# Six conversion steps per pair of heads: three and three between the halves, instead of two and four

## The chip, the cores and the metric

One core of one Trainium2 chip. The metric is the device time of one execution in microseconds (us); the kernel before takes 887.9 us. All runs of this study, of all kernels, agree with others of the same kernel to 0.3%, and none was in a slow state, so every comparison is between fast runs. Effects here are 0.1 to 0.7% of the time. I therefore read them twice: from timed runs, with an interval, and from intervals within the traces, which repeat far better (interval B, below, to about 0.04 us between kernels that should not differ in it).

## The reference

Attention whose mask comes from a hash, then a feed-forward layer:

```python
# q, k, v: (4, 8, 768, 64); proj: (64, 6)
q_bucket = number made of the 6 signs of q @ proj;  k_bucket likewise
scores = 0.125 * q @ k.T, masked (-1e9) where q_bucket != k_bucket
attn = softmax(scores);  x = (attn @ v) as (3072, 512)
# w_in: (512, 2048), w_out: (2048, 512), both float64
h = x @ w_in;  g = h / (1 + exp(-1.702 * h));  out = (g @ w_out).astype(float32)
```

`w_in` and `w_out` arrive as 64-bit numbers. The kernel computes in float32, so it turns each into a float32 number from its two 32-bit halves with a few operations: the "conversion" of this study. The reference computes in double precision there.

## The kernel before

The attention stage goes over 16 pairs of heads. Each pair is two groups, half c=0 and half c=1 of the queries. Of 16 chunks of `w_in` (128 x 512 numbers each), 14 are converted beside the attention, one in each of pairs 1 to 14, because VectorE has some time there; the last two are left to the feed-forward stage. In the traces VectorE and ScalarE take their operations in the order in which the program issues them: in the pair shown in the prediction, ScalarE begins the square L190 at 109.70, right behind L468, the operation before it in the program, though all that the square needs had been ready since 100.10. The parts that matter, cut:

```python
def convert(cv, dst, src, queue=None, psum=None):
    raw = cv.tile([P, CW, 2], U32, tag="raw", name="raw")
    (queue or loader[0]).dma_start(out=raw, in_=src)
    lo, hi = raw[:, :, 0], raw[:, :, 1]
    # ... here part is dst (SBUF) and size is hi, in place
    yield
    nc.vector.scalar_tensor_tensor(part, hi, 3, masks[0x3FFFFFFF], ...)          # L178
    yield
    nc.vector.scalar_tensor_tensor(bits, hi, 0xC0000000, part, ...)              # L182
    yield
    nc.vector.tensor_tensor(part, bits, masks[0xFF800000], op=Alu.bitwise_and)   # L186
    nc.scalar.activation(size, hi.bitcast(F32), Act.Square)                      # L190, ScalarE
    part = part.bitcast(F32)
    yield
    nc.vector.scalar_tensor_tensor(part, lo, 2.0**-52, part, ...)                # L193
    yield
    nc.vector.tensor_tensor(dst, of(bits.bitcast(F32)), of(part), op=Alu.add)    # L195
    yield
    nc.vector.scalar_tensor_tensor(dst, of(size), ..., dst, ...)                 # L198, needs the square
```

```python
def add_low(n, c):                       # GpSimd: the sum of exponentials 0 to 2
    nc.gpsimd.tensor_tensor(acc, es[c][:, 0, ...], es[c][:, 1, ...], op=Alu.add)  # L440
    nc.gpsimd.tensor_tensor(acc, acc, es[c][:, 2, ...], op=Alu.add)               # L441
def add_high(n, c):                      # VectorE: 3 to 5, and the other sum
    nc.vector.scalar_tensor_tensor(acc, e[0], T * TINY, e[1], ...)                # L446
    for x in (e[2], accs.pop((n, c, 0))):
        nc.vector.tensor_tensor(acc, acc, x, op=Alu.add)                          # L448
def unload(n, c):                        # ScalarE: av out of PSUM
    nc.scalar.copy(vs, av[:, HS : HS + 1])                                        # L467
    nc.scalar.activation(x_of(n)..., av..., Act.Identity, bias=vs[:, 0:1])        # L468
def total(n):                            # TensorE: denominators of both halves
    for c in range(2):
        acc = accs.pop((n, c))
        for j in range(2):
            nc.tensor.matmul(dn[r0 : r0 + 32, :], ones[:, 0:32], acc[:, j, :], ...)  # L477
# ... the loop over groups g = (n, c):
    scores(n, c, kts)                    # TensorE L432, exponentials on ScalarE L433
    if kts[0] == 0: add_low(n, c)
    if hashes: featured(hashes.pop())    # VectorE L413, then eight small transfers
    if ended: add_high(*prev[:2])
    for x in turned: turn(n + 1, x); measure(n + 1, x)   # in c=0
    while norms: norm(norms.pop(0))      # VectorE L497, in c=1
    ... total(), invert()                # in c=0: dn, then L484 to L492
    values(*prev)                        # TensorE L456, av
    if ended: unload(*prev[:2])
    if "q" in turned: hashed(n + 1)      # TensorE L408
    if kts and kts[-1] == T - 1:
        step(n, 2 + 2 * c)               # L576: the next steps of this pair's conversion
        if c == 0 and n > last - len(x_sums):
            x_sums[n - last - 1]()       # one 128 x 1024 operation in pairs 12 to 15
        if c == 1: begin(n + 1)          # load of the next chunk
```

## Time and profile before

| | before |
|---|---|
| median of the first 3 runs | 887.87 us |
| span in the profile | 885.6 us |
| TensorE / VectorE / ScalarE / GpSimd busy | 98% / 82% / 35% / 36% |
| attention stage (ends with the last `av`) | up to 330.6 us |

In the profile a line "L190" is a line of the kernel; PE is TensorE, DVE VectorE, ACT ScalarE, POOL GpSimd. A bracket at the end of a timeline line is the idle time of the engine before it, with what ended it. The lines on the steady state are in the prediction below. One stretch that it only mentions is shown here: the idle times of TensorE in pair 1, where the pipeline is still filling. Timeline of the kernel before, TensorE, columns start, duration, engine, line, operation, tiles, form:

```profile
52.53 0.84 PE L477 MATMUL dn<-acc,ones 128*32 128x384 f32 x4
54.91 0.84 PE L477 MATMUL dn<-acc,ones 128*32 128x384 f32 x4 [1.54 <-DVE acc L448]
```

Half of pair 1's denominators run at 52.53. The other half waits until VectorE ends its sum at 54.86, and so TensorE is idle for 1.54 us after the first half has ended.

### The profile page before, as it was taken

What the parts mean: (1) busy time and instruction counts of PE and PEld (TensorE: products, weight loads), DVE (VectorE), ACT (ScalarE), POOL (GpSimd) and SP (SyncE); (2) the same over time, 40 slices, a digit from 0 to 9 for tenths busy, and PEclk for the clock granted to TensorE, in tenths of its full rate; (3) what the DMA queues carried; (4) which work ended last, traced back from release to release, by engine and by line L of the source; (5) the groups of instructions that cost most, each with busy time, mean ns of one, the idle gap of its engine ahead of it and who ended that gap; (6) DMA issues with size and microseconds to landing.
All of it is one profiled execution on the core that took longest, in us unless ns stands there. A gap on an engine that the chain in (4) does not pass through costs nothing.

```text
span 885.6 us, 11940 instructions
## 1 busy us (share of the span) xinstructions
PE 869.4 (98%) x4077; PEld 501.0 (57%) x4077; DVE 723.3 (82%) x1020; ACT 309.2 (35%) x519; POOL 320.7 (36%) x275
## 2 busy tenths in 40 slices
PE   9999999999999999999999999999999999999995
PEld 5444444444444444444444444444888888888884
DVE  4599899999999965777778877888898977897785
ACT  5755666666656642223222223322000000000000
POOL 4244333433433363766434444559932000000000
PEclk9999999999999999999999999999999999999998
DMA  4754555566544103555455545575835665467524
GB/s 103 115 90 82 82 92 95 91 100 98 92 83 83 46 1 120 201 192 192 162 202 207 197 167 189 192 252 180 307 139 191 205 215 205 164 209 238 190 95 98
DMA packets 169477, 132.01 MB, mean 149 GB/s; under 512 B 123936, under 2 KB 138432, under 8 KB 164032
## 3 DMA queue, kind: packets, MB, share of 16 engines
q1 hardware_dynamic: 167712, 129.69, 51.5%
q10 hardware_dynamic: 1696, 1.48, 0.6%
q8 instruction: 34, 0.56, 0.3%
q14 instruction: 35, 0.29, 0.1%
HBM read 79.69 MB, written 50.33 MB: 147 GB/s over the span
## 4 chain that ended last, share of the span: by engine, by line
PE 96%; DVE 2%; ACTq 0%; ACT 0%; issue 0%; DVEq 0%
PE product L699 33%; PE product L812 28%; PE ps L432 17%; PE av L456 14%; PE dn L477 2%; PE hash L408 1%; PE tp L366 1%; DVE acc L448 0%; ACTq L420 0%; DVE xT L816 0%; PE warm L359 0%; PE hash L373 0%; DVE y L791 0%; DVE w_in_sb L193 0%; DVE w_in_sb L186 0%
## 5 line engine op out<-in xcount | busy, mean ns | idle before, releaser
L433 ACT ACTIVATE e<-ps 128x768 f32<-128x768 f32 x192 | 148.4, 811 | 23.5 <-PE ps L432 18.3
L432 PE MATMUL ps<-qT,kT 64*128 64x384 f32 x768 | 155.1, 482 | 0.0
L699 PE MATMUL product<-xT,w_in_sb 128*128 128x512 f32 x288 | 135.4, 592 | 0.0
L456 PE MATMUL av<-e,v 128*64 128x385 f32 x768 | 131.8, 490 | 0.9 <-ACT xT L468 0.9
L440 POOL TENSOR_TENSOR acc<-e 128x768 f32<-128x768 f32 x32 | 58.7, 1833 | 195.4 <-DVE acc L448 185.9
L707 ACT ACTIVATE c<-c 128x512 f32<-128x512 f32 x72 | 45.3, 630 | 186.4 <-issue 73.2
L456 PEld LDWEIGHTS av<-e,v 128*64 128x64 f32 x768 | 52.1, 136 | 77.6 <-issue 75.5
L699 PEld LDWEIGHTS product<-xT,w_in_sb 128*128 128x128 f32 x288 | 54.6, 190 | 68.5 <-issue 63.5
L699 PE MATMUL product<-t_x,s_in 128*128 128x512 f32 x192 | 90.2, 592 | 0.0
L432 PEld LDWEIGHTS ps<-qT,kT 64*128 64x128 f32 x768 | 68.2, 188 | 34.1 <-issue 32.9
L219 POOL TENSOR_TENSOR v<-c,u 128x512 f32<-128x512 f32 x24 | 34.2, 1423 | 127.5 <-ACT c L707 127.5
L818 ACT COPY u<-product 128x256 f32<-128x256 f32 x21 | 7.8, 372 | 168.0 <-PE product L812 125.8
L432 PE MATMUL ps<-qf,kf 64*128 64x384 bf16 x384 | 63.0, 324 | 1.3 <-ACT e L433 1.2
L699 PEld LDWEIGHTS product<-t_x,s_in 128*128 128x128 f32 x192 | 36.5, 190 | 45.9 <-issue 43.8
L441 POOL TENSOR_TENSOR acc<-acc,e 128x768 f32<-128x768 f32 x32 | 59.1, 1847 | 2.5
L699 PE MATMUL product<-t_x,w_in_sb 128*128 128x512 f32 x96 | 45.1, 592 | 0.0
L699 PE MATMUL product<-xT,s_in 128*128 128x512 f32 x96 | 45.1, 592 | 0.0
L432 PEld LDWEIGHTS <-kf 64*128 64x128 bf16 x384 | 20.1, 94 | 42.9 <-issue 21.4
L467 ACT COPY vs<-av 128x1 f32<-128x1 f32 x32 | 5.1, 159 | 91.1 <-PE av L456 91.1
L446 DVE SCALAR_TENSOR_TENSOR acc<-e 128x768 f32<-128x768 f32 x32 | 30.5, 953 | 7.7 <-ACT e L433 7.7
L812 PE MATMUL product<-raw_g,xT 128*128 128x256 f32 x152 | 35.1, 379 | 0.0
L448 DVE TENSOR_TENSOR acc<-acc,e 128x768 f32<-128x768 f32 x32 | 32.0, 999 | 2.4
(207 smaller groups left out, 1547.4 us busy)
## 6 DMA issues: line engine op xcount, KB each, us to landing
raw_g<-g_dram SPq DMA_DIRECT2D x22, 1024.0 KB
s_in<-g_dram SPq DMA_DIRECT2D x20, 1024.0 KB
g_dram<-c SPq DMA_DIRECT2D x72, 256.0 KB
g_dram<-t SPq DMA_DIRECT2D x48, 256.0 KB
raw<-in_moe_w_out_dram SPq DMA_DIRECT2D x16, 512.0 KB
raw<-in_moe_w_in_dram SPq DMA_DIRECT2D x15, 512.0 KB
v<-in_v_dram SPq DMA_DIRECT2D x32, 192.0 KB
g_dram<-u SPq DMA_DIRECT2D x24, 256.0 KB
```

What stands on the lines that cost most here:

```text
L219: return [lambda: eng.tensor_tensor(t1, b12, b11, op=Alu.subtract), lambda: eng.tensor_tensor(b12, b22, b12, op=Alu.subtract), lambda: eng ...
L432: nc.tensor.matmul(ps[:, j, 0:HS], a[hs, keys], m[hs, cols], start=not last, stop=last)
L433: nc.scalar.activation(es[c][:, kt, :, 0:HS], ps[:, :, 0:HS], Act.Exp, scale=1.0 / D**0.5)
L440: nc.gpsimd.tensor_tensor(acc, es[c][:, 0, :, 0:HS], es[c][:, 1, :, 0:HS], op=Alu.add)
L441: nc.gpsimd.tensor_tensor(acc, acc, es[c][:, 2, :, 0:HS], op=Alu.add)
L446: nc.vector.scalar_tensor_tensor(acc, e[0], T * TINY, e[1], op0=Alu.add, op1=Alu.add)
L448: nc.vector.tensor_tensor(acc, acc, x, op=Alu.add)
L456: nc.tensor.matmul(av[D * j : D * (j + 1), :], vt[:, t, j, :], es[c][:, t, j, :], start=(t == 0), stop=(t == T - 1))
L477: nc.tensor.matmul(dn[r0 : r0 + 32, :], ones[:, 0:32], acc[:, j, :], start=True, stop=True)
L699: nc.tensor.matmul(ps, wq[LEFT[i]][:, kc, :], xq[RIGHT[i]][:, kc, :], start=(kc == 0), stop=(kc == K2 - 1))
L707: nc.scalar.activation(c, c, Act.Gelu_apprx_sigmoid)
L812: nc.tensor.matmul(ps, wq[LEFT[i]][:, c, :], gq[RIGHT[i]][:, c, :], start=(c == 0), stop=(c == F4 - 1))
```

## The change

The half c=0 now takes three of the six remaining steps, and c=1 the other three. The intent is to share VectorE's work more evenly between the halves.

```diff
                 if kts and kts[-1] == T - 1:
-                    step(n, 2 + 2 * c)
+                    step(n, 3)
```

No work is added or removed. The third step holds L186 (VectorE) and L190 (ScalarE); these two move from c=1 to c=0, 14 times.

## The prediction

> **What bounds the kernel now.** I read the page first, for the engine that is never idle, then the chain of work that ended last, for the places where that engine is nevertheless late, then the waits, and last the timeline of one pair of heads (two groups: half c=1 of one pair, half c=0 of the next).
>
> ```profile
> PE   9999999999999999999999999999999999999995
> DVE  4599899999999965777778877888898977897785
> ```
>
> These are rows of the page, one digit per fortieth of the 885.6 us span. TensorE is full nearly everywhere. VectorE is almost full too, but only in slices 2 to 14, which is the attention stage (about 20 to 330 us) that the change touches. From 55 to 311 us the table by stages gives TensorE busy for all of every stretch, so no plain wait is left to take away there. What can be lost is hidden inside matmuls, so I compared equal groups along the chain:
>
> ```profile
> 34.99 0.78 PE dn L477 x8
> ...
> 54.91 0.84 PE dn L477 x4
> ...
> 113.94 0.97 PE dn L477 x8
> ...
> 311.45 1.13 PE dn L477 x8
> ...
> 342.79 0.78 PE dn L477 x8
> ```
>
> Columns: start, length on the chain in us, engine, tile, line, number. The same eight denominator matmuls (`dn`, once per pair) cost 0.78 us where nothing holds them and 0.96 to 1.14 us in pairs 2 to 14. The first four use the sum `acc` of half c=0, long ready; the other four use that of half c=1 and run beside them in other columns of the array, so a late second `acc` lengthens the group instead of showing as a gap. Why it is late, from the waits and the timeline:
>
> ```profile
> DVE w_in_sb L198 <- ACT raw L190: 10.3, 10, 1.0
> ```
>
> ```profile
> 103.65 0.95 DVE L497 TENSOR_TENSOR xT<-xT,rs 128x768 f32<-128x768 f32 x1
> 103.88 2.13 POOL L440 TENSOR_TENSOR acc<-e 128x768 f32<-128x768 f32 x1 [6.13 <-DVE acc L448]
> ...
> 104.52 2.03 DVE L186 TENSOR_TENSOR w_in_sb<-bits,mask_ff 128x512 uint32<-128x512 uint32 x1
> ...
> 106.08 2.01 POOL L441 TENSOR_TENSOR acc<-acc,e 128x768 f32<-128x768 f32 x1
> ...
> 106.59 2.05 DVE L193 SCALAR_TENSOR_TENSOR w_in_sb<-raw,w_in_sb 128x512 f32<-128x512 uint32 x1
> ...
> 109.22 0.58 ACT L468 ACTIVATE xT<-av,vs 128x384 f32<-128x384 f32 x1
> 109.70 0.66 ACT L190 ACTIVATE raw<-raw 128x512 f32<-128x512 f32 x1
> ...
> 110.40 0.69 DVE L198 SCALAR_TENSOR_TENSOR w_in_sb<-raw,w_in_sb 128x512 f32<-128x512 f32 x1 [1.03 <-ACT raw L190]
> ...
> 113.05 0.96 DVE L448 TENSOR_TENSOR acc<-acc,acc 128x768 f32<-128x768 f32 x1
> 113.86 1.04 PE L477 MATMUL dn<-acc,ones 128*32 128x384 f32 x8
> ```
>
> Here is a loop. ScalarE stands in order: its square L190 comes behind the unloading of `av` (L468), which waits for TensorE to end `av` at 108.98. So L198 starts only at 110.40, the last `acc` ends at 114.01, and `dn` ends about 0.89 us after that (114.90), where TensorE alone would have ended it at 113.94 + 0.78 = 114.72. TensorE thus waits 0.18 us per pair for a chain it started itself 5 us earlier. In pairs 12 to 14 the excess is 0.35 us and L198 does not wait: there VectorE has one x sum (1.22 us) more per pair and is simply full.
>
> **What the Trainium skill says.** "SBUF — State Buffer", section "SBUF: two separate sides", calls the port pair that VectorE and GpSimd share an exclusive lock: of a VectorE operation with two SBUF inputs and a GpSimd operation, the first holds it for the whole instruction and the other blocks. The trace agrees. L440 (1.54 us in the c=0 half) takes 2.13 behind L497; L186 takes 2.03 behind L440 although L182 and L195, of the same size, take 0.69; L193 takes 2.05 behind L441. "Perfetto Trace Analysis", section "Per-instruction lifecycle", says that the reported window of a VectorE operation starts with its execution, after its semaphores are met; the blocked time nevertheless lies inside the 2.03 us here, so a long operation may be a blocked one. "DMA: Bandwidth & Descriptors", section "Anatomy of one DMA", gives about 2 us of fixed cost per transfer; I use it only for the rival of the features.
>
> **The change part by part.** It removes and adds no work. A conversion has seven steps; the first begins at the end of the pair before. Then two were taken in half c=0 and four in c=1; now three and three. The listing of the two programs' orders shows that on each engine only this moves, 14 times (pairs 1 to 14): VectorE's L186 goes from behind L497 to right behind L182, ahead of the feature operation L413; ScalarE's L190 goes from behind the unloading in c=1 to behind that in c=0. TensorE, GpSimd and the DMA queue keep their order.
>
> 1. The wait of L198: 1.03 us of VectorE per pair in pairs 2 to 11 (10.3 us). Gone; the square is now made 10 us earlier.
> 2. L186 in its new place: GpSimd is idle there (L441 of c=0 ends at 117.46, L182 at 119.83), so 0.69 us instead of 2.03.
> 3. But L193 then stands behind L440 and L195 behind L441: L195 becomes about 2.0 us. The blocked time passes to the next operation; VectorE's busy time hardly changes. It is 19.72 - 1.03 = 18.69 us per pair, for a TensorE period of 4 groups and `dn`, `hash`: 2 x 4.95 + 2 x 4.03 + 0.78 + 0.78 = 19.52.
> 4. The feature operation L413: VectorE's `rt` (L484) may now start when `dn` ends (114.72 + 0.06), where it started at 115.68 before. From there to L413 were 4.11 us; with L186 it is 4.80: 119.58, just about where TensorE ends `hash` (119.53). So L413 stays in its place against TensorE.
> 5. From L413 to the end of the second `acc`: 114.01 - 100.07 = 13.94 before, less 0.69 and 1.03: 12.2 us. So `acc` is ready about 1.5 us before TensorE wants it, and `dn` falls to 0.78.
>
> Sum over the chain: pairs 2 to 11 have four times 0.97 and six times 0.96, 9.64 - 10 x 0.78 = 1.84 us. Pairs 12 to 14: 1.12 + 1.14 + 1.13 - 3 x 0.78 = 1.05; the x sums eat the spare time (about 0.8 us per pair against 1.13 us for a sum), and I estimate that about 0.3 us of lateness is left at pair 14, so 0.75. Pair 1, where `dn` waits for VectorE from 52.5 to 54.9: the chain there is VectorE's own work, of unchanged sum; only a wait of 0.1 us ends, so 0 to 0.1. Total about 2.6 us of 887.87. The feed-forward part (from 331 us) is TensorE after TensorE and only moves forward.
>
> **The rivals.**
> (a) ScalarE is put ahead of itself. The square now stands before the six exponentials of half c=1, and it waits for L182. In the steady state the unloading ends at 119.75 and the first score at about 120.7, so 0.66 us just fits. In pair 1 VectorE is late (L182 ends at 41.36, the exponentials started at 40.05): they would start about 2 us later, and with three score buffers TensorE stops for about 2 us near 41 us. That takes the place of its 2.4 us stop at 52.5 us and should cost nothing; if it costs, up to 2 us: 885 to 887.5. If 0.66 us did not fit in the steady state, 0.2 to 0.4 us per pair would give the gain back: 887 to 890.
> (b) L186 is slow by itself, not by the lock, and takes 2.03 us in its new place. Then L413 comes 1.4 us later, VectorE is full in pairs 12 to 14, and the features' eight issues (0.73 us each) land later. In pair 2 of the trace L413 started 6.3 us before the scores and they did not wait; here 7.5 us would be left. Gain about 2.2 us: 885.7.
> (c) L195 blocked by L441 delays more than I think, because the lock passes in another order. There are 1.5 us to spare; 886 at worst.
> (d) `dn` is long for another reason than `acc` (for example, port or clock): nothing moves, 887.9. Against it: 0.78 in pairs 0 and 15.
> (e) VectorE's freed 1 us is worth 14 us. Against it: it is off TensorE's path but for the excess above; TensorE has no more to give.
>
> **Range and chances.** Predicted 885.2 us. The whole excess of `dn` in pairs 2 to 14 is 2.89 us, and pair 1 adds at most about 2, so below 884 only something unseen leads. Above, (a) and (c) lead to 887. Two per cent would be 17.8 us, six times all that `dn` loses: within 2% is nearly sure.
>
> **What would show it.** L198 no longer waits for L190; L190 stands before the c=1 exponentials; L186 takes 0.69, L193 stays at 2.05, L195 grows to about 2.0; `dn` is 0.78 in pairs 2 to 12 on the chain, and a pair takes 19.52 us instead of 19.72; a new stop of TensorE near 41 us replaces that at 52.5. It is wrong if `dn` keeps its 0.96 though L198 waits for nothing, if scores wait for exponentials in every pair, or if the scores of a pair wait for the features.

## The result, and the profile after

The changed kernel takes 885.34 us (median of 6 fast runs, 884.88 to 885.63) against 887.86 (6 runs). The ratio is 0.9971, with a 95% interval of 0.9958 to 0.9984. Ratios in this document are those that the measuring program gives for the fast runs; they are not quite the ratios of the medians. The gain is clear of noise and far below 2%.

The chain that ended last, changed kernel, same columns as in the prediction:

```profile
54.45 1.42 PE dn L477 x8
...
113.69 0.78 PE dn L477 x8
...
269.97 0.78 PE dn L477 x8
...
289.51 0.97 PE dn L477 x8
...
309.23 1.19 PE dn L477 x8
...
340.63 0.78 PE dn L477 x8
```

Pairs 2 to 12 (74.62 to 269.97) all have 0.78 us now; only pairs 13 and 14 are still late. The timeline of one pair shows why:

```profile
98.50 0.69 DVE L182 SCALAR_TENSOR_TENSOR bits<-raw,w_in_sb 128x512 uint32<-128x512 uint32 x1
...
99.23 0.69 DVE L186 TENSOR_TENSOR w_in_sb<-bits,mask_ff 128x512 uint32<-128x512 uint32 x1
...
99.69 0.66 ACT L190 ACTIVATE raw<-raw 128x512 f32<-128x512 f32 x1
...
103.65 2.13 POOL L440 TENSOR_TENSOR acc<-e 128x768 f32<-128x768 f32 x1 [7.53 <-DVE acc L448]
...
104.29 2.03 DVE L193 SCALAR_TENSOR_TENSOR w_in_sb<-raw,w_in_sb 128x512 f32<-128x512 uint32 x1
...
105.85 2.01 POOL L441 TENSOR_TENSOR acc<-acc,e 128x768 f32<-128x768 f32 x1
...
106.36 2.05 DVE L195 TENSOR_TENSOR w_in_sb<-bits,w_in_sb 128x512 f32<-128x512 f32 x1
108.52 0.69 DVE L198 SCALAR_TENSOR_TENSOR w_in_sb<-raw,w_in_sb 128x512 f32<-128x512 f32 x1
...
111.25 0.96 DVE L448 TENSOR_TENSOR acc<-acc,acc 128x768 f32<-128x768 f32 x1
```

The square is made at 99.69, nearly 9 us before L198. L198 has no bracket: it waits for nothing, and in the list of waits it no longer appears. The last `acc` of the pair ends at 112.21, well before `dn` wants it at 113.69. L186 takes 0.69 us in its new place, and L193 and L195 now take the two long places beside GpSimd's L440 and L441.

In pair 1 TensorE's stop has moved. Timeline of the changed kernel:

```profile
41.45 0.67 ACT L190 ACTIVATE raw<-raw 128x512 f32<-128x512 f32 x1 [2.53 <-DVE bits L182]
...
42.87 0.34 PE L432 MATMUL ps<-qf,kf 64*128 64x384 bf16 x2 [1.61 <-ACT e L433]
```

ScalarE waits 2.53 us for VectorE's late L182 before it can make the square; the exponentials stand behind it, the score buffers stay full, and TensorE stops for 1.61 us.

The start of an execution differs by up to about 1 us between profiled runs of all kernels (the hash of pair 2 starts between 37.45 and 38.61 us), so spans of single profiles don't compare to 0.1 us. The ends differ too: in the ten traces TensorE's last matmul ends 532.5 to 532.7 us after the start of pair 15's `dn`, but the execution ends 9.7 to 11.4 us after that. I use two intervals within each trace: A, from the start of pair 2's `hash` (in pair 1) to the end of pair 1's `dn`, and B, from there to the start of pair 15's `dn`. "x8" or "L186 0.69" below are from the same traces.

| kernel | time, us | ratio to before (95%) | A, us | B, us |
|---|---|---|---|---|
| before | 887.86 | 1 | 17.94 | 287.04 |
| changed | 885.34 | 0.9971 (0.9958 to 0.9984) | 18.00 | 284.76 |
| square alone moved | 884.71 | 0.9970 (0.9958 to 0.9982) | 17.87 | 284.76 |
| L186 alone moved | 887.76 | 1.0000 (0.9992 to 1.0008) | 17.70 | 287.02 |
| square ahead of the unloading | 884.91 | 0.9971 (0.9960 to 0.9982) | 17.92 | 284.56 |
| changed, pair 1 as before | 884.24 | 0.9963 (0.9950 to 0.9977) | 17.94 | 284.76 |
| conversions one pair later | 882.74 | 0.9948 (0.9935 to 0.9962) | 15.56 | 284.76 |
| x sums in every second pair | 884.58 | 0.9961 (0.9947 to 0.9974) | 18.00 | 284.16 |
| both | 881.56 | 0.9933 (0.9920 to 0.9947) | 15.57 | 284.17 |
| all six steps in half c=0 | 885.45 | 0.9972 (0.9960 to 0.9983) | 17.98 | 284.72 |

The kernel before ran in each of the three sets: 887.86, 887.61 and 887.77 us.

### The profile page after: what moved, and what is told of

It is laid out like the page before. It is cut to its first block, busy times and chain, and to the rows that moved or that the text cites. A ratio compares the mean times of both kernels' runs of the same rounds, so it can differ in the third digit from the quotient of the medians.

```text
span 883.4 us, 11926 instructions
## 1 busy us (share of the span) xinstructions
PE 866.9 (98%) x4077; PEld 498.4 (56%) x4077; DVE 724.9 (82%) x1020; ACT 313.3 (35%) x519; POOL 319.9 (36%) x275
## 3 DMA queue, kind: packets, MB, share of 16 engines
q10 hardware_dynamic: 1696, 1.48, 0.6%
## 4 chain that ended last, share of the span: by engine, by line
PE 96%; DVE 1%; DMA 1%; ACTq 0%; issue 0%; POOL 0%; ACT 0%; SPq 0%; POOLq 0%; DVEq 0%
PE product L699 33%; PE product L812 28%; PE ps L432 17%; PE av L456 14%; PE dn L477 1%; PE hash L408 1%; DMA q<-in_q_dram 1%; PE tp L366 1%; ACTq L420 0%; DVE xT L816 0%; PE hash L373 0%; DVE y L791 0%; SPq L328 0%; DMA qf<-f 0%; DVE rs L492 0%
## 5 line engine op out<-in xcount | busy, mean ns | idle before, releaser
L433 ACT ACTIVATE e<-ps 128x768 f32<-128x768 f32 x192 | 150.9, 811 | 18.4 <-PE ps L432 12.4
L440 POOL TENSOR_TENSOR acc<-e 128x768 f32<-128x768 f32 x32 | 58.6, 1832 | 193.3 <-DVE acc L448 166.3
L441 POOL TENSOR_TENSOR acc<-acc,e 128x768 f32<-128x768 f32 x32 | 59.0, 1845 | 2.5
L446 DVE SCALAR_TENSOR_TENSOR acc<-e 128x768 f32<-128x768 f32 x32 | 30.5, 954 | 7.7 <-ACT e L433 7.7
L448 DVE TENSOR_TENSOR acc<-acc,e 128x768 f32<-128x768 f32 x32 | 32.0, 999 | 3.3
```

Of the source, the lines that this page charges most:

```text
L433: nc.scalar.activation(es[c][:, kt, :, 0:HS], ps[:, :, 0:HS], Act.Exp, scale=1.0 / D**0.5)
L440: nc.gpsimd.tensor_tensor(acc, es[c][:, 0, :, 0:HS], es[c][:, 1, :, 0:HS], op=Alu.add)
L441: nc.gpsimd.tensor_tensor(acc, acc, es[c][:, 2, :, 0:HS], op=Alu.add)
L446: nc.vector.scalar_tensor_tensor(acc, e[0], T * TINY, e[1], op0=Alu.add, op1=Alu.add)
```

## The experiments

All results were correct, all runs fast. The first four kernels shared a chip and the runs of before, and so did the last four. In the first three, what was added stands on existing or empty lines as far as it could, so that line numbers stay.

### Which of the two moves brings the gain?

**Only the square is moved.** VectorE keeps two and four.

```diff
-        nc.vector.scalar_tensor_tensor(bits, hi, ...)                     # L182
+        nc.vector.scalar_tensor_tensor(bits, hi, ...); nc.scalar.activation(size, hi.bitcast(F32), Act.Square)
         yield
...
-        nc.scalar.activation(size, hi.bitcast(F32), Act.Square)           # L190
```

(only in the conversions beside the attention, as in the next two kernels; with `step(n, 2 + 2 * c)`)

> Two steps and four as before on VectorE (L186 stays in half c=1), but the square of ScalarE alone is moved to half c=0, behind L182. My theory (the loss was the loop: end of av, unloading, square, L198, acc, dn): L198 waits for nothing, dn falls to 0.78 us in pairs 2 to 12, the gain of the whole change is there: 885.3 us, about 2.5 below the kernel before. L186 and L193 keep 2.0 us each, L195 stays 0.69. The stop of TensorE near 41 us in pair 1 is there too (the square waits for L182). Rival (the gain comes from VectorE's L186 out of GpSimd's shadow): nothing gained, 887.9 us, dn stays at 0.96.

Measured: 884.71 us, ratio 0.9970, B 284.76 us as in the changed kernel. Its timeline (the square is at L182 here):

```profile
99.23 0.67 ACT L182 ACTIVATE raw<-raw 128x512 f32<-128x512 f32 x1
...
103.82 2.03 DVE L186 TENSOR_TENSOR w_in_sb<-bits,mask_ff 128x512 uint32<-128x512 uint32 x1
...
105.89 2.05 DVE L193 SCALAR_TENSOR_TENSOR w_in_sb<-raw,w_in_sb 128x512 f32<-128x512 uint32 x1
107.98 0.69 DVE L195 TENSOR_TENSOR w_in_sb<-bits,w_in_sb 128x512 f32<-128x512 f32 x1
...
108.77 0.69 DVE L198 SCALAR_TENSOR_TENSOR w_in_sb<-raw,w_in_sb 128x512 f32<-128x512 f32 x1
...
113.16 0.85 PE L477 MATMUL dn<-acc,ones 128*32 128x384 f32 x8
```

VectorE's steps stand as before, L186 as long as before, and `dn` is short all the same (in the timeline 0.85, where 1.04 stood; on the chain 0.78). The whole gain is here.

**Only L186 is moved.** VectorE's order is that of the changed kernel; the square stays in c=1, behind the unloading.

```diff
-                    step(n, 2 + 2 * c)
+                    step(n, 3)
...
-        nc.scalar.activation(size, hi.bitcast(F32), Act.Square)           # L190
         part = part.bitcast(F32)
-        yield
+        yield; nc.scalar.activation(size, hi.bitcast(F32), Act.Square)    # L192
```

> VectorE's order as in the changed kernel (L186 in half c=0), but the square stays in half c=1 behind the unloading. My theory: L198 still waits about 1.0 us for the square in pairs 2 to 11, dn stays at 0.96 us, nothing gained: 887.8 us; L186 0.69 us, L195 2.05 us all the same; no stop of TensorE at 41 us, that at 52.5 us stays. Rival (L186's place brings the gain): 885.3 us, dn at 0.78.

Measured: 887.76 us, ratio 1.0000, B 287.02 us: nothing. Its timeline:

```profile
106.88 2.06 DVE L195 TENSOR_TENSOR w_in_sb<-bits,w_in_sb 128x512 f32<-128x512 f32 x1
...
109.31 0.66 ACT L192 ACTIVATE raw<-raw 128x512 f32<-128x512 f32 x1
110.00 0.69 DVE L198 SCALAR_TENSOR_TENSOR w_in_sb<-raw,w_in_sb 128x512 f32<-128x512 f32 x1 [1.06 <-ACT raw L192]
```

L198 waits 1.06 us for the square and `dn` keeps 0.96. The more even share of VectorE's steps is worth nothing by itself. A is 0.24 us shorter than before, because VectorE ends pair 1's `acc` that much sooner in this run; the timed runs don't show it, and the reason (a load that landed earlier) is given below, under "Why the prediction was right".

**The square only ahead of the unloading.** The steps stay two and four, and the square stays in half c=1; it only changes places with the unloading of `av` on ScalarE.

```diff
+        if square == 0: nc.scalar.activation(size, hi.bitcast(F32), Act.Square); yield    # L184
...
+                if c == 1 and kts[-1] == T - 1: step(n)
                 if ended:
                     unload(*prev[:2])
```

> Two steps and four as before, all in half c=1; only the square goes ahead of the unloading of av on ScalarE instead of behind it. My theory: the square runs right behind the exponentials, some 3 us earlier, L198 waits for nothing, dn 0.78 us in pairs 2 to 12 and 0.2 and 0.4 us above that in pairs 13 and 14; in pair 1 TensorE stops at 52.5 us as before (2.4 us) and not at 41. Time 885.4 us. Rival (the half in which the steps stand is what counts): 887.9 us.

Measured: 884.91 us, ratio 0.9971, B 284.56 us. Its timeline:

```profile
105.86 0.68 ACT L184 ACTIVATE raw<-raw 128x512 f32<-128x512 f32 x1
...
109.37 0.58 ACT L468 ACTIVATE xT<-av,vs 128x384 f32<-128x384 f32 x1
109.63 0.69 DVE L198 SCALAR_TENSOR_TENSOR w_in_sb<-raw,w_in_sb 128x512 f32<-128x512 f32 x1
```

The square now runs 3.5 us before the unloading, L198 waits for nothing, and `dn` is 0.78 in pairs 2 to 12 (0.82 and 1.13 in 13 and 14). It is the place of the square behind an operation that waits for TensorE, not the half or the share of steps, that cost the time. A rival that no run separates: the square also stood before the exponentials of the next half, which began 0.35 us after their first score in the kernel before and begin 0.10 us after it in the changed one. The timeline of the kernel before leaves no room for it, since no score waits there, and VectorE has no bracket from L198 to the end of the last `acc`. This version has no stop at 41 us in pair 1; it has the old one of 1.52 us before the second half of `dn`.

### Does the new stop in pair 1 cost anything?

**The changed kernel with pair 1 as before.**

```diff
-                    step(n, 3)
+                    step(n, 3 if n > 1 else 2 + 2 * c)
```

> The changed kernel, but pair 1 keeps two and four. My theory: the stop of 1.6 us near 41 us (scores wait for exponentials behind the square) goes away and that of about 2.4 us at 52.5 us comes back, since VectorE's chain up to the end of acc at 54.9 us sets the end in both: time 885.3 us as the changed kernel, within 0.3 us. Rival (the stop at 41 us costs): 883.7 us.

Measured: 884.24 us, ratio 0.9963 (interval 0.9950 to 0.9977). The stop near 41 us is gone, and the one before `dn` is back at 1.54 us. A is 17.94 us against 18.00 in the changed kernel, and B the same. My theory had 885.3 within 0.3 us and so missed the median by 1.1 us; the rival's 883.7 is nearer. But the changed kernel ran in another set; the kernel with the square alone, which stops near 41 us too and ran in this one, took 884.71, and the intervals don't part the two. The traces do: 0.06 us, not 1.6. VectorE runs without a wait from its transpose of pair 2's q (L391) to the end of pair 1's last `acc`, and takes 18.54 us for that here (36.55 to 55.09) and 18.61 in the changed kernel (36.37 to 54.98). The two stops are the same lateness of VectorE, met at two places.

**Every conversion one pair later**, in pairs 2 to 15, so that pair 1 has none.

```diff
-                if n - 1 < len(in_chunks) - LATE:
-                    conv[n] = convert(cv, *in_chunks[n - 1], nc.sync if n > 1 else nc.scalar)
+                if 1 < n <= last:
+                    conv[n] = convert(cv, *in_chunks[n - 2], nc.sync)
```

> The changed kernel with every conversion one pair later (pairs 2 to 15 instead of 1 to 14), so pair 1, where VectorE is behind, has none. My theory: TensorE's stop in pair 1 (1.6 us near 41 us and a dn of 1.42) is VectorE's work and vanishes; pair 15 has no transposes of a next pair and room for the steps; about 2.4 us gained: 882.9 us. Pairs 13 and 14 keep their 0.2 and 0.4 us. Rival (the stop is the start-up's features and exponentials): 885.3 us.

Measured: 882.74 us, ratio 0.9948. A falls from 18.00 to 15.56 us, 2.44 us less, B is unchanged. Chain:

```profile
52.30 0.78 PE dn L477 x8
```

With no steps in pair 1, TensorE runs through the whole pair without a stop, and pair 1's `dn` takes 0.78 us. The edit takes the whole conversion out of pair 1, the square on ScalarE too, and issues the first chunk's load from SyncE instead of ScalarE; these are not tested apart. That the stop was VectorE's work is read from the other traces, where it ends with VectorE's `acc` or `bits`. Pair 15 takes the last conversion without a loss.

### What is left in pairs 13 and 14?

**The x sums in every second pair.** These four operations (1.22 us each) may start once the first eight pairs are done.

```diff
-                    if c == 0 and n > last - len(x_sums):
-                        x_sums[n - last - 1]()
+                    if c == 0 and n in (9, 11, 13, 15):
+                        x_sums[(n - 9) // 2]()
```

> The changed kernel with the four x sums (1.22 us of VectorE each) in pairs 9, 11, 13, 15 instead of 12 to 15. My theory: VectorE has about 0.6 us to spare per pair, so one sum in every second pair is made up for by the next pair; dn is 0.78 us in pairs 2 to 14, 0.6 us gained: 884.7 us. Rival (the long dn of pairs 13 and 14 has another cause): 885.3 us, dn of 13 and 14 as before.

Measured: 884.58 us, ratio 0.9961; B 284.16, 0.60 us below the changed kernel's. The interval of the ratio doesn't part 0.6 us from nothing; the chain does:

```profile
290.10 0.78 PE dn L477 x8
...
309.63 0.78 PE dn L477 x8
```

Pairs 13 and 14 had 0.97 and 1.19. They were late because VectorE, with three such operations in a row, was fuller than TensorE; one pair without a sum makes up for it.

**Both of these together.**

> Both of the two others: conversions in pairs 2 to 15 and x sums in 9, 11, 13, 15. If both theories hold the gains add: 882.3 us, 5.5 us below the kernel before.

Measured: 881.56 us, ratio 0.9933 (0.9920 to 0.9947). A is 15.57 and B 284.17 us: the two gains add, to 5.24 us in A + B below the kernel before. This version beats both kernels. Between 29.6 us and the end of the attention stage, TensorE has one idle stretch left, 0.9 us for the unloading of the last pair.

### Is three and three a special share?

**All six steps in half c=0.**

```diff
-                    step(n, 3)
+                    step(n, 6 - 6 * c)
```

> All six steps in half c=0, none in c=1. My theory: once the square is out of the loop the split does not matter: 885.3 us, dn 0.78 us in pairs 2 to 12. L186, L193, L195 and L198 take 0.69 us each, and the lock's delay passes to the next operations with two SBUF inputs in half c=1: the sums L446 and L448 of c=1 take about 2 us instead of 0.95. L413 starts 2.1 us later than in the changed kernel, the features still land in time. Rival (three and three is the point): 887 us or more; or the features land late and the scores of each pair wait: over 889 us.

Measured: 885.45 us, ratio 0.9972; A 17.98 and B 284.72, as in the changed kernel. All four steps that had been moved take 0.69 us, and the long places beside GpSimd are taken by others:

```profile
106.54 2.12 POOL L440 TENSOR_TENSOR acc<-e 128x768 f32<-128x768 f32 x1 [9.72 <-DVE acc L448]
107.19 2.30 DVE L446 SCALAR_TENSOR_TENSOR acc<-e 128x768 f32<-128x768 f32 x1
108.74 2.27 POOL L441 TENSOR_TENSOR acc<-acc,e 128x768 f32<-128x768 f32 x1
...
109.59 2.25 DVE L448 TENSOR_TENSOR acc<-acc,e 128x768 f32<-128x768 f32 x1
111.94 0.96 DVE L448 TENSOR_TENSOR acc<-acc,acc 128x768 f32<-128x768 f32 x1
```

L446 and L448 of half c=1 take 2.30 and 2.25 us instead of 0.95 and 0.96. The share of the steps does not matter once the square is out of the way. The features, whose operation starts 2.3 us later against TensorE's scores than before the change, made no scores wait.

## Why the prediction was right

The measured 885.34 us lies 0.14 us from the predicted 885.2. By the traces the gain has the cause that the prediction gives. That the number is so near is partly luck: it counted on about 2.6 us, the traces show 2.22 in A + B, and the medians happen to differ by 2.5.

- **Wait of L198** (step 1): gone, as said. That this wait was the loss in pairs 2 to 11 is shown from both sides: the square alone brings the whole gain (B 284.76), L186 alone nothing (B 287.02). In pairs 12 to 14 L198 did not wait before either; there the timelines show that VectorE, which with an x sum needs 19.96 us per pair (L413 at 257.26 and 277.22) against TensorE's 19.53, now starts some 1.5 us ahead and falls behind later.
- **L186 in its new place** (step 2): 0.69 us, as said, so rival (b) is out.
- **The delay passes on** (step 3): L193 2.03 and L195 2.05 us, as said. With six steps in c=0 it passes on to L446 and L448. VectorE's busy time hardly changed (723.3 us before, 724.9 after).
- **Feature operation** (step 4): L413 starts at 119.37, `hash` ends at 119.29; the time from L484 to L413 is 4.83 us where 4.80 was worked out.
- **From L413 to the last `acc`** (step 5): 12.37 us (99.84 to 112.21), a little more than the 12.2 worked out: the 1.03 us of waiting did not go entirely, as from the end of L195 to the start of L198 there were 1.04 us and still are 0.11. `acc` is ready 1.48 us before `dn`, about 1.5 as said (the prediction's own sums give 1.7). The spare time of VectorE, seen as the wait of L484 for `dn`, is 0.6 us per pair, where I had put 0.8. So the x sums left more lateness than I said: pairs 12, 13 and 14 stand at 0.78, 0.97 and 1.19, 0.60 us above their floor together, where I had estimated 0.3. This is the term of the sum that was mis-sized; the 1.13 us that it sets for an x sum is 1.22 in the trace and elsewhere in the same text. The chain gains 2.89 - 0.60 = 2.29 us in pairs 2 to 14, and A + B together fall by 2.22 us.
- **Rival (a)** in pair 1: the stop near 41 us came (1.61 us) and took the place of the old one; it costs 0.06 us in A. The old stop was misread as 2.4 us: that is the distance from the first half of `dn` to the second (52.53 to 54.91), and TensorE is idle for 1.54 of it. The wait of 0.1 us that was to end in pair 1 is still there (L195 to L198: 0.10 before, 0.11 after). In the steady state the square fitted between the unloading and the first exponential, as L433's start at 100.78 right after the first score shows: no scores wait for exponentials there.
- **Rivals (c), (d) and (e)**: the order of the lock left 1.5 us to spare; `dn` fell with the wait; and 1 us of VectorE per pair did not become more than TensorE had been losing.

One reading of the page was wrong without harm: VectorE's row shows 8 and 9 not only in the attention stage but in many slices after it.

Interval A of the kernel with L186 alone, 0.24 us shorter than before, has an outside cause. In pair 1 TensorE waits for VectorE, and VectorE's chain begins when the load of pair 2's q has landed (L391 waits for it: 1.37 us before the change, 1.27 here). L391 starts 1.72 us before `hash` here and 1.49 before the change; from there to the end of the last `acc` it is 18.52 and 18.54 us. Over all kernels with a conversion in pair 1 this chain takes 18.52 to 18.54 us with the old stop and 18.59 to 18.63 with the new one, so the new stop costs under 0.1 us.

What stays open: the timed median of the kernel with pair 1 as before is 1.1 us below the changed kernel's, from another set of runs, and no interval of the traces shows that.

## What to carry to other kernels

When the bound engine shows no gap, compare equal groups of its work along the chain: a group that takes 0.96 us where its twin takes 0.78 is waiting inside. Then follow the late operand back until the chain meets the bound engine itself; such a loop is cut by taking a short operation on an in-order engine out from behind one that waits for the bound engine, which here was worth all of the change, while sharing the work more evenly was worth nothing. An operation that is long beside GpSimd gets short when moved (L186: 2.03 to 0.69 us), but here the delay went to the next operations with two inputs in SBUF (L195: 0.69 to 2.05; with all six steps moved, L446 and L448).

## What the Trainium skill lacked or had wrong

- "Perfetto Trace Analysis", section "Optimization Strategy", advises to look for the gaps between slices on the bound engine. Here the loss was in no gap: TensorE counts as busy for 254.00 of 254 us from 56 to 310 us in both kernels, though a pair takes 19.72 us in one and 19.53 in the other. It shows as a group of eight matmuls of 0.96 us instead of 0.78, half of whose operands are late.
- "Perfetto Trace Analysis", section "Per-instruction lifecycle", has the reported window of a VectorE operation start with its execution. Waiting for the port shared with GpSimd lies inside the reported time: L186 is 2.03 us beside GpSimd and 0.69 us away from it, with no idle time shown before it.
- "SBUF — State Buffer", section "SBUF: two separate sides", agrees with the traces shown here on the exclusive lock, and on operations with two SBUF inputs, `scalar_tensor_tensor` among them (L446: 0.95 to 2.30 us). It does not say what every run here shows that moves such an operation: while GpSimd's work stays, moving the blocked operation saves nothing, as the next one with two SBUF inputs takes over the delay (L186 less 1.34 us, L195 more by 1.36).
- No page draws what follows when an engine keeps its order: an operation that is free to run can stand behind one that waits for the bound engine, and so delay that engine. The square, free to run over 9 us earlier (L182, the last that it needs, ends at 100.10 and it starts at 109.70), cost TensorE 0.18 us in each of ten pairs.
